# Gate column copied ahead of the masks, V three tiles ahead, query product first: a change to the prologue of a fused gated attention and feed-forward kernel

## The chip, the cores and the metric

The kernel runs on one core of one Trainium2 chip. The metric is the device time of one execution in microseconds (us), as the median of several executions. A run counts as slow, and is left out of the ratios, when it lies over 1.5% above the fastest of its kernel. The profiled span is about 2.0 to 2.3 us shorter than the time, because it runs from the first to the last recorded instruction of one execution.

## The reference

The input is x of 2048 rows and 512 columns (bf16). One branch is linear attention with 32 heads of 16, whose feature map is a pair of softmaxes; the other is a feed-forward layer with 1376 hidden units. A sigmoid gate mixes them.

```python
g = sigmoid((x * gate_w).sum(-1, keepdims=True))
# branch A
q, k, v = split(x @ wqkv)                      # 32 heads of 16
pq = einsum("bhsd,hdf->bhsf", q, w_phi)        # the same w_phi for k
phi_q = concat([softmax(pq), softmax(-pq)])    # phi_k alike
kv = einsum("bhsf,bhsd->bhfd", phi_k, v);  z = phi_k.sum(over s)
o = (phi_q @ kv) / (phi_q @ z + 1e-6)
a = o @ wo
# branch B
b = relu(x @ w1) @ w2
out = g * a + (1 - g) * b
```

## The kernel before

Each engine has its own list of instructions, executed in order; an event (`ev`) is a semaphore count that a later instruction waits for (`after`). The parts that matter here are all in the prologue. Three words are used throughout: a load "lands" when its data have arrived; a "bubble" is time by which a matmul starts later than the pace of its forerunners allows; "filler" is other work put where PE would wait. A hidden unit (`hunit`) and a V tile (`vtile`) are four matmuls of 512 columns each; the feed-forward layer takes eleven hidden units for 512 rows.

The loads go out from one queue (SP) in this order: x of the first 512 rows, W1 in pieces, the gate row, the rest of W1, the V weights (`WV`), the small w_phi (`WPS`), then the query and key weights **transposed** (`WQKT`), then the other rows of x.

```python
for dt in range(NDT):
    load_w1(1, dt)
p.dma("sp", ... GWR <- gate_w ..., ev="gwr")
p.dma("sp", ... W1[:, :, 1024:DFF] <- B_w1 ..., ev="w1r")
p.dma("sp", ... WV <- A_wqkv[:, 2 * D:3 * D] ..., ev="wv")
p.dma("sp", ... WPS <- A_w_phi ..., ev="wps")
p.dma("sp", lambda e: e.dma_start_transpose(out=WQKT, in_=A_wqkv[:, 0:2 * D]), "wqk", ev="wqk")
```

On DVE four block-diagonal masks times w_phi (`Wbd`) are emitted early, so they precede the gate column's copy, which makes the gate row a 97th column of the last hidden unit's weights:

```python
for gt in range(NDT):                       # emitted first
    p.op("dve", ... Wbd[:, gt, :] = WPS * M16 ..., after=["wps", "m16"], ev=f"wbd{gt}")
# ... cut ...
def gatecol():                              # emitted later
    p.op("pe",  ... transpose of GWR into PS[:, 3] ..., ev="gwt")
    p.op("dve", ... W1[:, :, DFF:DFF + 1] <- PS[:, 3] ..., after=["gwt"], ev="gw3")
```

`pre` multiplies the transposed weights with the masked w_phi, so that queries and keys come out of one projection already mapped ("merged weights"): eight groups of four small matmuls, the first four for queries, the last four for keys. Each group is copied out of PSUM (`pc0` to `pc7`), even ones by DVE and odd ones by ACT.

```python
def pre(half):
    PB = [0, 1, 2, 7]
    for i in range(4 * half, 4 * half + 4):
        # four matmuls  PS[:, PB[i % 4]] = WQKT * Wbd   after wqk, wbd0..3, a free bank
        # copy to WqP or WkP, ev=f"pc{i}"
```

The first tile of projections waits for all eight copies; query and key matmuls alternate. V tiles run two ahead.

```python
def atile(m):
    first = xready(m // 4) + ([f"em{m - 1}"] if m >= 1 else [f"pc{i}" for i in range(8)])
    pairs = [(dt, which) for dt in range(NDT) for which in (1, 0)]   # 1 = key, 0 = query
```

The order of PE work:

```python
hfirst(1, 0); gatecol(); hfirst(1, 1); hfirst(1, 2); hfirst(1, 3)
hunit(0, KTO[8])          # the hidden unit with the gate column, waits for gw3
hunit(0, KTO[9])
vtile(0)
pre(0)
hunit(0, KTO[10])
pre(1)
vtile(1)
for m in range(NT):       # 16 tiles
    atile(m)              # 8 matmuls, then exponentials (ACT), sums (DVE), scaling (POOL)
    if m >= LAG: kv(m - LAG)
    if m in vt: vtile(vt[m])
    for _ in range(nh[m]): hnext()     # one to three hidden units as filler
```

A tile with `nh[m] == 1` has its exponentials split so that the next tile's keys can start before its queries are done. After the loop come the products with kv, the output projections and the mixing.

The softmax here doesn't subtract the row's maximum and nothing guards it: scores larger than these inputs give would overflow.

## Time and profile before

| | before |
|---|---|
| median of runs | 153.9 us (153.61 to 153.94) |
| profiled span | 151.4 us |
| PE busy | 145.9 us, 96% of the span |
| first query/key projection starts | 20.44 us |

From the page of the kernel before: the span, the busiest engine, the busy tenths of the DMA engines in 40 slices of 3.8 us, and the chain of waits by engine.

```profile
span 151.4 us, 2399 instructions
...
PE 145.9 (96%) x925; PEld 73.9 (49%) x942; DVE 90.1 (59%) x147; ACT 79.8 (53%) x131; POOL 52.5 (35%) x57
...
DMA  4999993883533304333333311622223222332232
...
PE 87%; DMA 6%; SPq 4%; issue 1%; DVE 0%
```

PE is the bound, and the 16 DMA engines are 90% busy or more in the slices from 3.8 to 22.7 us, while the loads come in. Where PE stands idle is seen in its timeline. Columns: start in us, time in us, engine, line, operation, output<-inputs, shapes, number of merged instructions, and in brackets the idle time before it and what ended it.

```profile
10.22 0.17 PE L278 MATMUL PS<-IDN,GWR 4*128 4x4 bf16 x1
...
13.71 1.93 PE L258 MATMUL PS<-XT,W 128*97 128x512 bf16 x8 [0.61 <-DVE W L281]
15.47 1.03 PE L377 MATMUL PS<-WV,XT 128*128 128x512 bf16 x4
16.75 1.07 PE L294 MATMUL PS<-Wbd,PHQ 128*128 128x128 bf16 x16 [0.25 <-DMA PHQ<-in_A_wqkv_dram]
17.66 1.03 PE L258 MATMUL PS<-XT,W 128*128 128x512 bf16 x4
18.52 1.06 PE L294 MATMUL PS<-Wbd,PHQ 128*128 128x128 bf16 x16
19.63 0.81 PE L377 MATMUL PS<-WV,XT 128*128 128x512 bf16 x3
20.44 0.38 PE L321 MATMUL PS<-WkP,XT 128*128 128x512 bf16 x1
```

The timeline of DVE in the same stretch, the same columns:

```profile
12.67 0.90 DVE L234 TENSOR_TENSOR Wbd<-WPS,M 128x128 bf16<-128x128 bf16 x4 [5.22 <-DMA WPS<-in_A_w_phi_dram]
13.48 0.17 DVE L281 COPY W<-PS 128x4 bf16<-128x4 bf16 x1
```

The chain of waits of the kernel before, in order of time (start, length, what), around its last piece that is not PE:

```profile
7.42 9.28 DMA PHQ<-in_A_wqkv_dram
16.71 0.05 issue
16.75 1.07 PE PS L294 x16
```

How to read this. Matmuls of 512 columns start 0.216 us apart when nothing holds them, although each is shown as 0.38 us long. The Trainium skill (Perfetto Trace Analysis, "Tensor Engine Instruction") says that a matmul's end in a profile is estimated from its size and the memory's delay, not observed; the trace agrees in that matmuls which start 0.216 us apart are shown overlapping. So the idle time in brackets understates a bubble by 0.38 - 0.216 = 0.16 us. From start to start the bubbles are 0.77 us before 13.71 us (the gate copy on DVE, stuck behind four mask products that waited for w_phi until 12.67 us), 0.42 us before 16.75 us (the transposed load, which lands at 16.71 us), and 0.16 us before 20.44 us (the last copies of the merged weights). After that PE has no bubble until the tail. The V tile at 19.63 us shows three of its four matmuls: some records are missing from a trace (925 of PE here).

### The profile page before, as it was taken

What the parts mean: (1) busy time and instruction counts of PE and PEld (TensorE: products, weight loads), DVE (VectorE), ACT (ScalarE), POOL (GpSimd) and SP (SyncE); (2) the same over time, 40 slices, a digit from 0 to 9 for tenths busy, and PEclk for the clock granted to TensorE, in tenths of its full rate; (3) what the DMA queues carried; (4) which work ended last, traced back from release to release, by engine and by line L of the source; (5) the groups of instructions that cost most, each with busy time, mean ns of one, the idle gap of its engine ahead of it and who ended that gap; (6) DMA issues with size and microseconds to landing.
All of it is one profiled execution on the core that took longest, in us unless ns stands there. A gap on an engine that the chain in (4) does not pass through costs nothing.

```text
span 151.4 us, 2399 instructions
## 1 busy us (share of the span) xinstructions
PE 145.9 (96%) x925; PEld 73.9 (49%) x942; DVE 90.1 (59%) x147; ACT 79.8 (53%) x131; POOL 52.5 (35%) x57
## 2 busy tenths in 40 slices
PE   7998999999999999999999999999999999999993
PEld 2843544444445454444544445444444444445472
DVE  0502555777868786686688788455554555444462
ACT  3356649987787888878788763311222111111141
POOL 2000005987786686788668653000000000000000
PEclk9999999999999999999999999999999999999999
DMA  4999993883533304333333311622223222332232
GB/s 132 288 246 232 218 177 70 325 244 69 74 69 71 69 19 80 47 69 69 69 76 69 69 28 42 138 71 72 69 69 74 69 69 72 86 88 70 75 96 74
DMA packets 42130, 15.57 MB, mean 103 GB/s; under 512 B 37160, under 2 KB 41384, under 8 KB 42120
## 3 DMA queue, kind: packets, MB, share of 16 engines
q1 hardware_dynamic: 41448, 13.49, 40.5%
q0 software_dynamic: 528, 1.93, 3.7%
q8 instruction: 7, 0.11, 0.3%
q10 hardware_dynamic: 144, 0.01, 0.1%
q14 instruction: 3, 0.02, 0.0%
HBM read 4.41 MB, written 2.10 MB: 43 GB/s over the span
## 4 chain that ended last, share of the span: by engine, by line
PE 87%; DMA 6%; SPq 4%; issue 1%; DVE 0%
PE PS L467 23%; PE PS L258 19%; PE PS L321 18%; PE PS L479 9%; PE PS L377 8%; DMA PHQ<-in_A_wqkv_dram 6%; PE PS L438 3%; PE PS L399 3%; SPq L138 2%; PE PS L505 2%; PE PS L294 1%; PE PS L516 1%; SPq L148 1%; SPq L160 0%; SPq L158 0%
## 5 line engine op out<-in xcount | busy, mean ns | idle before, releaser
L467 PE MATMUL PS<-W,HT 128*128 128x512 bf16 (+1 forms) x159 | 37.6, 380 | 0.3
L258 PE MATMUL PS<-XT,W 128*128 128x512 bf16 (+1 forms) x142 | 34.3, 380 | 0.7 <-DVE W L281 0.6
L358 POOL TENSOR_TENSOR FM<-FM,SC 128x1024 bf16<-128x1024 bf16 x15 | 28.9, 1929 | 13.2 <-DVE SC L343 13.2
L484 ACT ACTIVATE TFA<-PS,GT 128x512 bf16<-128x512 f32 x15 | 10.3, 687 | 39.6 <-PE PS L479 39.6
L340 DVE TENSOR_REDUCE ZB<-FM 128x64 f32<-128x1024 bf16 x16 | 19.5, 1220 | 17.4 <-ACT FM L332 15.2
L273 ACT ACTIVATE HT<-PS 128x512 bf16<-128x512 f32 (+1 forms) x44 | 24.8, 608 | 8.6 <-PE PS L258 4.3
L332 ACT ACTIVATE FM<-PS 128x1024 bf16<-128x1024 f32 x22 | 21.3, 1021 | 10.1 <-PE PS L321 10.1
L467 PEld LDWEIGHTS PS<-W,HT 128*128 128x128 bf16 (+1 forms) x165 | 16.0, 98 | 19.6 <-ACT HT L273 0.3
L321 PE MATMUL PS<-WqP,XT 128*128 128x512 bf16 x64 | 22.3, 380 | 0.1
L321 PE MATMUL PS<-WkP,XT 128*128 128x512 bf16 x63 | 21.9, 379 | 0.0
L258 PEld LDWEIGHTS PS<-XT,W 128*128 128x128 bf16 (+1 forms) x144 | 14.0, 101 | 16.1 <-DVE W L281 1.1
L351 DVE TENSOR_REDUCE ZB<-FM 128x64 f32<-128x1024 bf16 x16 | 18.7, 1168 | 0.0
L363 POOL TENSOR_TENSOR FM<-FM,SC 128x512 bf16<-128x512 bf16 x16 | 16.9, 1054 | 1.3
L444 DVE RECIPROCAL RDEN<-PS 128x32 f32<-128x32 f32 x16 | 5.7, 357 | 17.6 <-PE PS L438 17.6
L490 DVE SCALAR_TENSOR_TENSOR OSB<-PS,OMG,TFA 128x512 bf16<-128x512 f32 x15 | 11.3, 751 | 7.1 <-ACT TFA L484 7.0
L377 PE MATMUL PS<-WV,XT 128*128 128x512 bf16 x58 | 15.1, 379 | 0.3
L479 PE MATMUL PS<-WO,OT 128*128 128x512 bf16 x59 | 15.0, 379 | 0.1
L337 ACT ACTIVATE FM<-PS 128x512 bf16<-128x512 f32 x20 | 10.3, 604 | 3.8 <-PE PS L321 3.8
L448 DVE TENSOR_TENSOR OTM<-PS,RDEN 128x512 bf16<-128x512 f32 x16 | 11.1, 691 | 0.6
L321 PEld LDWEIGHTS PS<-WkP,XT 128*128 128x128 bf16 x64 | 6.3, 98 | 7.9 <-DVE WkP L299 0.5
L321 PEld LDWEIGHTS PS<-WqP,XT 128*128 128x128 bf16 x64 | 6.3, 98 | 7.4
L343 DVE RECIPROCAL SC<-ZB 128x64 f32<-128x64 f32 x16 | 8.8, 553 | 0.5
(59 smaller groups left out, 106.5 us busy)
## 6 DMA issues: line engine op xcount, KB each, us to landing
out_dram<-OSB SPq DMA_DIRECT2D x15, 128.0 KB, 1.9
W<-in_B_w_dram POOLq DMA_DIRECT2D x1, 1280.0 KB, 6.6
W<-in_B_w_dram SPq DMA_DIRECT2D x8, 128.0 KB, 3.5
OT<-in_A_x_dram SPq DMA_DIRECT2D x2, 256.0 KB, 3.3
WV<-in_A_wqkv_dram SPq DMA_DIRECT2D x1, 512.0 KB, 6.0
WO<-in_A_wo_dram POOLq DMA_DIRECT2D x1, 512.0 KB, 7.0
W<-in_B_w_dram SPq DMA_DIRECT2D x1, 352.0 KB, 4.0
PHQ<-FM SPq DMA_TRANSPOSE x16, 2.7
```

The lines of the kernel that those rows point to most:

```text
L258: p.op("pe", lambda e, c=c, kt=kt, M=M, dt=dt, bank=bank: e.matmul(PS[0:M, bank, :], W1[:, dt, kt * P:kt * P + M], XT[:, dt, c * 512:(c + ...
L273: p.op("act", lambda e, c=c, kt=kt, Mr=Mr, bank=bank: e.activation(HT[0:Mr, kt, c * 512:(c + 1) * 512], PS[0:Mr, bank, :], ACT.Relu), afte ...
L321: p.op("pe", lambda e, m=m, dt=dt, which=which, W=(WqP, WkP)[which]: e.matmul(PS[:, which, :], XT[:, dt, m * P:(m + 1) * P], W[:, dt, :], ...
L332: p.op("act", lambda e, o=fm5[:, :, :, s, :], i=src, s=s: e.activation(o, i, ACT.Exp, scale=(1.0 if s == 0 else -1.0)), after=[f"qk{m}"] + ...
L340: p.op("dve", lambda e, b=b: e.tensor_reduce(ZB[:, b, 64:128], FM[:, b, 1, :].rearrange("p (g f) -> p g f", f=DH), AX.X, ALU.add), after=[ ...
L351: p.op("dve", lambda e, b=b: e.tensor_reduce(ZB[:, b, 0:64], FM[:, b, 0, :].rearrange("p (g f) -> p g f", f=DH), AX.X, ALU.add), after=[f" ...
L358: p.op("pool", lambda e, fk=fk, rk=rk: e.tensor_tensor(fk, fk, rk, ALU.mult), after=[f"rz{m}"], ev=f"pk{m}")
L363: p.op("pool", lambda e, b=b, fq=fq: e.tensor_tensor(fq, fq, SC[:, b, 0:32].unsqueeze(2).to_broadcast([P, H, DH]), ALU.mult), after=[f"sc{ ...
L377: p.op("pe", lambda e, m=m, dt=dt, bank=bank: e.matmul(PS[:, bank, :], XT[:, dt, m * P:(m + 1) * P], WV[:, dt, :], start=(dt == 0), stop=( ...
L467: p.op("pe", lambda e, kt=kt, M=M, m=m, bank=bank: e.matmul(PS[:, bank, :], HT[0:M, kt, m * P:(m + 1) * P], W2[0:M, kt, :], start=(kt == 0 ...
L479: p.op("pe", lambda e, t=t, m=m: e.matmul(PS[:, bank, :], OT[:, t, m * P:(m + 1) * P], WO[:, t, :], start=(t == 0), stop=(t == NDT - 1)), ...
L490: p.op("dve", lambda e, m=m, ob=ob: e.scalar_tensor_tensor(out=OSB[:, ob, :], in0=PS[:, BB[m % 3], :], scalar=OMG[:, m:m + 1], in1=TFA[:, ...
```

## The change

Its intent: to take the gate copy from behind the masks on DVE; to give PE work while it waits for the transposed load (a hidden unit before the merged weights, a third V tile after them); and to let the first projection begin with queries, which need only the first four copies. It needs a deeper V buffer (8 in place of 5), another assignment of PSUM banks, and it spreads the hidden units differently over the loop. The gate row's load goes out earlier (ahead of the second block of W1), and its transpose on PE comes four matmuls later.

```diff
@@
     GW = 128
     NB = 5
     NH = 3
+    NV = 8
     LAG = 3
 
     with ExitStack() as es:
@@
         W2 = E(nc.sbuf_tensor("W2", [P, KT, D], BF16))
         WO = E(nc.sbuf_tensor("WO", [P, NDT, D], BF16))
         FM = E(nc.sbuf_tensor("FM", [P, NB, 2, 2 * D], BF16))
-        VS = E(nc.sbuf_tensor("VS", [P, NB, NG, 68], BF16))
+        VS = E(nc.sbuf_tensor("VS", [P, NV, NG, 68], BF16))
         PHQ = E(nc.sbuf_tensor("PHQ", [P, NG, S], BF16))
         KVNZ = E(nc.sbuf_tensor("KVNZ", [P, NG, 68], BF16))
         OT = E(nc.sbuf_tensor("OT", [P, NDT, S], BF16))
@@
             load_w1(0, i)
         load_w1(0, 2)
         load_w1(0, 3)
+        p.dma("sp", lambda e: e.dma_start(out=GWR[:, :], in_=gate_w.rearrange("(j p) -> j p", p=P)), "gwr", ev="gwr")
         for dt in range(NDT):
             load_w1(1, dt)
-        p.dma("sp", lambda e: e.dma_start(out=GWR[:, :], in_=gate_w.rearrange("(j p) -> j p", p=P)), "gwr", ev="gwr")
         p.dma("sp", lambda e: e.dma_start(
             out=W1[:, :, 1024:DFF], in_=B_w1[:, 1024:DFF].rearrange("(j p) n -> p j n", p=P)), "w1r", ev="w1r")
         p.dma("sp", lambda e: e.dma_start(
@@
              after=["iota1", "r16"], ev="m16")
         p.op("dve", lambda e: e.tensor_tensor(M32[:, :], ROW32[:, 0:64], COL16[:, 0:64], ALU.is_equal),
              after=["r32"], ev="m32")
-        for b in range(NB):
+        for b in range(NV):
             p.op("dve", lambda e, b=b: e.memset(VS[:, b, :, 64:65], 1.0), ev=f"one{b}")
-        for gt in range(NDT):
-            wps_b = bass.AP(tensor=WPS, offset=gt * DH, ap=[[NDT * DH, P], [0, 8], [1, DH]])
-            p.op("dve", lambda e, gt=gt, a=wps_b: e.tensor_tensor(
-                Wbd[:, gt, :].rearrange("p (a b) -> p a b", a=8), a,
-                M16[:, :].rearrange("p (a b) -> p a b", a=8), ALU.mult),
-                after=["wps", "m16"], ev=f"wbd{gt}")
-
 
         hcount = [0]
 
@@
             p.op("dve", lambda e: e.tensor_copy(
                 W1[:, :, DFF:DFF + 1], PS[:, 3, 0:NDT].bitcast(BF16)[:, 0:NDT].unsqueeze(2)), after=["gwt"], ev="gw3")
 
+        def wbd():
+            # the four mask products removed above, unchanged
 
         def pre(half):
-            PB = [0, 1, 2, 7]
+            PB = [0, 1, 2, 7, 1, 2, 7, 3]
             for i in range(4 * half, 4 * half + 4):
                 which, dt = i // 4, i % 4
-                bank = PB[i % 4]
+                bank = PB[i]
                 dst = (WqP, WkP)[which]
-                after = ["wqk"] + [f"wbd{g}" for g in range(NDT)] + ([bfree[bank]] if i < 4 else [])
-                if i >= 4:
-                    after.append(f"pc{i - 4}")
+                after = ["wqk"] + [f"wbd{g}" for g in range(NDT)] + [f"pc{PB.index(bank)}" if PB.index(bank) < i else bfree[bank]]
                 for gt in range(NDT):
                     p.op("pe", lambda e, which=which, dt=dt, gt=gt, bank=bank: e.matmul(
                         PS[:, bank, gt * P:(gt + 1) * P], WQKT[:, which * NDT + gt, dt * P:(dt + 1) * P],
@@
                     p.op("act", lambda e, dst=dst, dt=dt, bank=bank: e.activation(
                         dst[:, dt, :], PS[:, bank, :], ACT.Copy), after=[f"pm{i}"], ev=f"pc{i}")
 
-        nh = [2, 2, 2, 2, 1, 2, 2, 1, 2, 2, 1, 2, 3, 1, 2]
+        nh = [2, 2, 2, 1, 2, 1, 2, 1, 2, 1, 2, 3, 3, 1, 2]
         split = [m for m in range(NT - 1) if nh[m] == 1] + [NT - 1]
 
         def atile(m):
@@
             if m >= 1:
                 first = first + [f"em{m - 1}"]
             else:
-                first = first + [f"pc{i}" for i in range(8)]
+                first = first + [f"pc{i}" for i in range(4)]
             after_split = m - 1 in split
             pairs = [(dt, which) for dt in range(NDT) for which in (1, 0)]
             if after_split:
                 pairs.sort(key=lambda t: -t[1])
                 first = [e for e in first if not e.startswith("em")] + [f"emk{m - 1}"]
+            mid = [f"em{m - 1}"] if after_split else ()
+            if m == 0:
+                pairs.sort(key=lambda t: t[1])
+                mid = [f"pc{i}" for i in range(4, 8)]
             for i, (dt, which) in enumerate(pairs):
                 p.op("pe", lambda e, m=m, dt=dt, which=which, W=(WqP, WkP)[which]: e.matmul(
                     PS[:, which, :], XT[:, dt, m * P:(m + 1) * P], W[:, dt, :],
                     start=(dt == 0), stop=(dt == NDT - 1)),
-                    after=(first if i == 0 else [f"em{m - 1}"] if after_split and i == NDT else ()),
+                    after=(first if i == 0 else mid if i == NDT else ()),
                     ev=(f"qk{m}" if i == 2 * NDT - 1 else None))
             fm5 = FM[:, b, :, :].rearrange("p a (h s f) -> p a h s f", h=H, s=2)
             src = PS[:, 0:2, :].rearrange("p a (h f) -> p a h f", h=H)
@@
                 f"tq{b}", after=[f"pq{m}"] + ([f"pm7"] if m == 12 else []), ev=f"tq{m}")
 
         def vtile(m):
-            b = m % NB
-            bank = 6 if m < 2 else 2
+            b = m % NV
+            bank = 6 if m < 3 else 2
             prev = [f"cv{m - 1}"] if m else [bfree[bank]]
-            if m == 2:
-                prev.append("pc6")
+            if m == 3:
+                prev.append("pc5")
             for dt in range(NDT):
                 p.op("pe", lambda e, m=m, dt=dt, bank=bank: e.matmul(
                     PS[:, bank, :], XT[:, dt, m * P:(m + 1) * P], WV[:, dt, :],
@@
                     after=((xready(m // 4) + ["wv"] + prev) if dt == 0 else ()),
                     ev=(f"v{m}" if dt == NDT - 1 else None))
             dst, src = VS[:, b, :, 0:64], PS[:, bank, :].rearrange("p (g c) -> p g c", g=NG)
-            after = [f"v{m}"] + ([f"kv{m - NB}"] if m >= NB else [])
-            if m < 2:
+            after = [f"v{m}"] + ([f"kv{m - NV}"] if m >= NV else [])
+            if m < 3:
                 p.op("dve", lambda e, d=dst, s=src: e.tensor_copy(d, s), after=after, ev=f"cv{m}")
             else:
                 p.op("act", lambda e, d=dst, s=src: e.activation(d, s, ACT.Copy), after=after, ev=f"cv{m}")
@@
             for g in range(NG):
                 after = []
                 if g == 0:
-                    after = [f"pka{m}" if m == NT - 1 else f"pk{m}", f"cv{m}", f"one{b}"]
+                    after = [f"pka{m}" if m == NT - 1 else f"pk{m}", f"cv{m}", f"one{m % NV}"]
                     if m == 0:
-                        after += ["cv1", "pc7"]
+                        after += ["cv2", "pc7"]
                 elif g == NG // 2 and m == NT - 1:
                     after = [f"pk{m}"]
                 p.op("pe", lambda e, m=m, b=b, g=g: e.matmul(
                     PS[:, 6 + g // 4, (g % 4) * GW:(g % 4) * GW + 65],
-                    FM[:, b, 1, g * P:(g + 1) * P], VS[:, b, g, 0:65],
+                    FM[:, b, 1, g * P:(g + 1) * P], VS[:, m % NV, g, 0:65],
                     start=(m == 0 and g % 4 == 0), stop=(m == NT - 1), skip_group_check=True),
                     after=after, ev=(f"kv{m}" if g == NG - 1 else f"kva{m}" if g == NG // 2 - 1 else None))
 
@@
         for kt in KTO[0:4]:
             hunit(0, kt, mm=False)
         hfirst(1, 0)
+        hfirst(1, 1)
         gatecol()
-        hfirst(1, 1)
+        wbd()
         hfirst(1, 2)
         hfirst(1, 3)
         for kt in KTO[4:8]:
@@
         hunit(0, KTO[8])
         hunit(0, KTO[9])
         vtile(0)
+        hunit(0, KTO[10])
         pre(0)
-        hunit(0, KTO[10])
+        vtile(1)
         pre(1)
-        vtile(1)
+        vtile(2)
+        bfree[3] = "pc7"
         units = [(c, kt) for c in range(1, NCH) for kt in [KT - 1] + list(range(KT - 1))]
-        vt = {m: m + 2 for m in range(NT - 4)}
+        vt = {m: m + 3 for m in range(NT - 5)}
         vt[NT - 3], vt[NT - 2] = NT - 2, NT - 1
 
         def hnext():
```

(Of the diff, the definition of the new `wbd()`, which holds the removed lines unchanged, and the line numbers are left out.)

More of the change, by code (lines that the diff above doesn't have):

```diff
@@ L282, in gatecol @@
                 W1[:, :, DFF:DFF + 1], PS[:, 3, 0:NDT].bitcast(BF16)[:, 0:NDT].unsqueeze(2)), after=["gwt"], ev="gw3")
+        def wbd():
+            for gt in range(NDT):
+                wps_b = bass.AP(tensor=WPS, offset=gt * DH, ap=[[NDT * DH, P], [0, 8], [1, DH]])
+                p.op("dve", lambda e, gt=gt, a=wps_b: e.tensor_tensor(
+                    Wbd[:, gt, :].rearrange("p (a b) -> p a b", a=8), a,
+                    M16[:, :].rearrange("p (a b) -> p a b", a=8), ALU.mult),
+                    after=["wps", "m16"], ev=f"wbd{gt}")
         def pre(half):
-            PB = [0, 1, 2, 7]
+            PB = [0, 1, 2, 7, 1, 2, 7, 3]
             for i in range(4 * half, 4 * half + 4):
                 which, dt = i // 4, i % 4
-                bank = PB[i % 4]
+                bank = PB[i]
                 dst = (WqP, WkP)[which]
-                after = ["wqk"] + [f"wbd{g}" for g in range(NDT)] + ([bfree[bank]] if i < 4 else [])
-                if i >= 4:
-                    after.append(f"pc{i - 4}")
+                after = ["wqk"] + [f"wbd{g}" for g in range(NDT)] + [f"pc{PB.index(bank)}" if PB.index(bank) < i else bfree[bank]]
                 for gt in range(NDT):
```

## The prediction

> What bounds the kernel. The profiled span is 151.4 us (153.9 us timed); the busy table puts PE at 96%, every other engine at 59% or less. In the timeline of PE, from the first query/key projection (20.44 us) on, matmuls of 512 columns start 0.216 us apart without a visible bubble; the chain of waits is almost all PE from 16.75 us. The Trainium skill (TensorE: Matmul & The Clock Gate, "Phases on the wall clock") gives about 216 ns per 512-column matmul back to back; the starts agree, and the 380 ns of the groups is latency. So only bubbles ahead of 20.44 us can be won.
>
> Bubbles there, from the starts of successive matmuls:
> 1. 12.93 to 13.71 us, 0.77 us: the hidden unit with the gate column waits for that column's copy (0.17 us), which sits on DVE behind four mask products (0.90 us), which wait until 12.67 us for their small weight load.
> 2. 16.34 to 16.75 us, 0.42 us: the merged weights wait for the transposed load of the query/key weights, landing at 16.71 us.
> 3. 20.28 to 20.44 us, 0.16 us: the first projection waits for the last copies of the merged weights (ACT, 20.29 us).
> Sum 1.35 us.
>
> What the change does. No matmul is added or removed. The gate copy now runs right after its transpose, about 11.3 us, well before 12.93; the mask products still end near 13.6 us, long before they are needed. Bubble 1 goes, but PE then meets the same landing of the transposed load, whose place in the queue is unchanged. A hidden unit (4 x 0.216 us) moves ahead as filler: work before the merged weights ends at 12.93 + 16 x 0.216 = 16.39 us, so bubble 2 stays at about 0.36 us. After 16.75 us, 32 small matmuls (0.056 us each) and two V tiles (0.86 us each) end at 20.27 us. Bubble 3 goes, because the query half needs only the first four copies (done about 18.5 us), and the key half starts 0.86 us later, when the others are done. I allow 0.05 us for V tile 2, which waits for the DVE copy of V tile 1 in the same bank.
> Before, the first projection started at 20.44 us with two V tiles done; after, at about 20.3 us with three. Gain: 0.14 + 0.86 = about 1.0 us, all on the critical path.
>
> Later parts. Six tiles instead of five have split exponentials. ACT in a one-unit iteration is about 2.06 + 0.6 + 0.6 us of 3.7 us of PE; POOL (1.93 + 0.25 + 1.05 us) and DVE (about 3.3 us) fit too. I expect no new bubble and no further gain.
>
> Prediction: 152.9 us, 8 in 10 between 152.3 and 153.5. Faster by over 2%: 0.02; within 2%: 0.96; slower by over 2%: 0.02.
>
> What would show it: no PE wait on the gate copy near 13 us; that copy ahead of the mask products on DVE; PE waiting about 0.36 us for the query/key weight load, still landing near 16.7 us; the first projection near 20.3 us, query first; then an unbroken chain and a span near 150.4 us.
>
> What would make it wrong: the transposed load landing at another time, which the merged weights follow one to one; a stall of V tile 2 or of the key half behind DVE copies; a wait on exponentials in the alternating one-unit iterations (3, 5, 7, 9), where ACT has least room; first-chunk matmuls waiting for weights now issued 0.4 us later, behind the gate row.

## The result, and the profile after

| | before | after |
|---|---|---|
| median of runs | 153.91 us (4 runs, 153.61 to 153.94) | 153.01 us (4 runs, 152.91 to 153.24) |
| profiled span | 151.4 us | 150.8 us |
| merged products start | 16.75 us | 17.13 us |
| first projection starts, V tiles done by then | 20.44 us, two | 20.72 us, three |

The ratio is 0.9948, with a 95% interval of 0.9931 to 0.9965: a small gain clear of the noise, well within 2%.

The page of the changed kernel, the same lines:

```profile
span 150.8 us, 2422 instructions
...
PE 146.5 (97%) x942; PEld 74.1 (49%) x942; DVE 90.8 (60%) x151; ACT 79.5 (53%) x132; POOL 52.6 (35%) x57
...
DMA  4999995793433319133333311622222223332232
...
PE 87%; DMA 6%; SPq 4%; issue 1%; DVE 0%
```

Its timeline of PE:

```profile
10.87 0.17 PE L272 MATMUL PS<-IDN,GWR 4*128 4x4 bf16 x1
...
12.71 1.89 PE L252 MATMUL PS<-XT,W 128*97 128x512 bf16 x8
14.44 1.03 PE L381 MATMUL PS<-WV,XT 128*128 128x512 bf16 x4
15.30 1.03 PE L252 MATMUL PS<-XT,W 128*128 128x512 bf16 x4
17.13 1.07 PE L294 MATMUL PS<-Wbd,PHQ 128*128 128x128 bf16 x16 [0.80 <-DMA PHQ<-in_A_wqkv_dram]
18.04 1.03 PE L381 MATMUL PS<-WV,XT 128*128 128x512 bf16 x4
18.90 1.06 PE L294 MATMUL PS<-Wbd,PHQ 128*128 128x128 bf16 x16
19.85 1.04 PE L381 MATMUL PS<-WV,XT 128*128 128x512 bf16 x4
20.72 1.03 PE L325 MATMUL PS<-WqP,XT 128*128 128x512 bf16 x4
21.59 1.03 PE L325 MATMUL PS<-WkP,XT 128*128 128x512 bf16 x4
```

Its timeline of DVE:

```profile
11.08 0.18 DVE L275 COPY W<-PS 128x4 bf16<-128x4 bf16 x1 [3.80 <-PE PS L272]
13.05 0.90 DVE L281 TENSOR_TENSOR Wbd<-WPS,M 128x128 bf16<-128x128 bf16 x4 [1.79 <-DMA WPS<-in_A_w_phi_dram]
```

Its chain of waits:

```profile
7.37 9.72 DMA PHQ<-in_A_wqkv_dram
17.09 0.05 issue
17.13 1.07 PE PS L294 x16
```

The gate copy now runs at 11.08 us, the gate unit at 12.71 us without a wait. The first projection begins with queries, at 20.72 us, and keys follow without a wait at 21.59 us. But the wait at the merged products is 0.97 us from start to start, not 0.36 us: the load landed at 17.09 us in this execution, 0.38 us later than in the profile of before, and PE reached the spot at 16.17 us, 0.22 us earlier than estimated. That is why the two spans differ by only 0.6 us while the medians differ by 0.9 us. Whether the later landing belongs to the change or to this one execution was the first question for the chip.

### The profile page after: what moved, and what is told of

Its sections match the earlier page's. It is cut to its first block, busy times and chain, and to the rows that moved or that the text cites. A ratio compares the mean times of both kernels' runs of the same rounds, so it can differ in the third digit from the quotient of the medians.

```text
span 150.8 us, 2422 instructions
## 1 busy us (share of the span) xinstructions
PE 146.5 (97%) x942; PEld 74.1 (49%) x942; DVE 90.8 (60%) x151; ACT 79.5 (53%) x132; POOL 52.6 (35%) x57
## 4 chain that ended last, share of the span: by engine, by line
PE 87%; DMA 6%; SPq 4%; issue 1%; DVE 0%
PE PS L471 24%; PE PS L252 19%; PE PS L325 18%; PE PS L381 9%; PE PS L483 9%; DMA PHQ<-in_A_wqkv_dram 6%; PE PS L442 3%; PE PS L403 3%; SPq L139 2%; PE PS L509 2%; PE PS L294 1%; PE PS L520 1%; SPq L149 1%; SPq L161 0%; SPq L159 0%
## 5 line engine op out<-in xcount | busy, mean ns | idle before, releaser
L471 PE MATMUL PS<-W,HT 128*128 128x512 bf16 (+1 forms) x165 | 38.1, 379 | 0.0
L336 ACT ACTIVATE FM<-PS 128x1024 bf16<-128x1024 f32 x20 | 19.4, 1021 | 8.6 <-PE PS L325 8.6
L325 PE MATMUL PS<-WkP,XT 128*128 128x512 bf16 x64 | 21.3, 379 | 0.0
L325 PE MATMUL PS<-WqP,XT 128*128 128x512 bf16 x64 | 21.3, 379 | 0.0
L381 PE MATMUL PS<-WV,XT 128*128 128x512 bf16 x64 | 16.4, 379 | 0.0
L341 ACT ACTIVATE FM<-PS 128x512 bf16<-128x512 f32 x24 | 12.4, 602 | 4.7 <-PE PS L325 4.7
L173 POOL DMA_DIRECT2D W<-in_B_w_dram x1 | 1.1, 1127 | 24.0 <-DMA XT<-in_A_x_dram 24.0
```

Of the source, the lines that this page charges most:

```text
L325: p.op("pe", lambda e, m=m, dt=dt, which=which, W=(WqP, WkP)[which]: e.matmul(PS[:, which, :], XT[:, dt, m * P:(m + 1) * P], W[:, dt, :], ...
L336: p.op("act", lambda e, o=fm5[:, :, :, s, :], i=src, s=s: e.activation(o, i, ACT.Exp, scale=(1.0 if s == 0 else -1.0)), after=[f"qk{m}"] + ...
L341: p.op("act", lambda e, o=fm5[:, which, :, s, :], i=src[:, which], s=s: e.activation(o, i, ACT.Exp, scale=(1.0 if s == 0 else -1.0)), afte ...
L381: p.op("pe", lambda e, m=m, dt=dt, bank=bank: e.matmul(PS[:, bank, :], XT[:, dt, m * P:(m + 1) * P], WV[:, dt, :], start=(dt == 0), stop=( ...
L471: p.op("pe", lambda e, kt=kt, M=M, m=m, bank=bank: e.matmul(PS[:, bank, :], HT[0:M, kt, m * P:(m + 1) * P], W2[0:M, kt, :], start=(kt == 0 ...
```

## The experiments

All kernels gave correct results. Theory A, from the prediction: the merged products start when the transposed load lands or when PE gets there, whichever is later, and nothing after them has a bubble in the new order. Its rivals are that each bubble is worth its own length, or that the change itself delays the load. Runs of one group shared a chip and its runs of the kernel before.

### The changed kernel again (after_again, no edit)

> The changed kernel once more, unedited, for the spread of the landing of the transposed query/key load. Theory A (the merged weights start at that landing and nothing after it has a bubble): the load lands somewhere between 16.6 and 17.2 us, the merged weights start 0.04 us later, the first projection 3.6 us after that; ratio to before 0.993 to 0.996. Rival (the change itself made the load land 0.4 us later, because the gate row now goes ahead of block 1): the landing stays at 17.1 us or later in every profile of a kernel with the gate row ahead.

Measured: 152.76 us (152.35 to 153.14), ratio 0.9902 (0.9847 to 0.9956). The ratio is below the one expected because five of the eleven runs of before on this chip lay near 155 us; against the other runs under 154 us (median 153.41 us) the gain is 0.65 us. The same line of PE's timeline as above:

```profile
16.50 1.07 PE L294 MATMUL PS<-Wbd,PHQ 128*128 128x128 bf16 x16
```

PE reached the merged products at 16.40 us by the count of starts and waited 0.10 us at most: the load had landed by 16.46 us, earlier than the 16.6 us expected, with the gate row ahead in the queue. So the rival, that the change makes the load land at 17.1 us or later, falls. In the other profiles that waited for the uncut load, the merged products started between 16.46 and 17.13 us with the gate row early, and between 16.75 and 16.88 us with it late. The second thing that moves is PE's arrival. In the profiles of before_again, old_units and split_load_2 (below) the matmuls' pace doubled (128 columns from 0.107 to 0.056 us apart) at about 3.9, 4.4 and 6.7 us. The Trainium skill (TensorE: Matmul & The Clock Gate, Part 1, "What's actually happening") says that the array's clock is held at half until a window of activity has passed, and that this window does not start with the kernel, so the moment varies from run to run. These traces agree that it varies; here it does so by 2.8 us, more than the half microsecond to either side that the page gives there. A late rise goes with a late arrival, though not strictly: the transpose of the gate row ran at 10.39 us in old_units (rise at 4.4 us), at 11.31 us in split_load_2 (6.7 us), but at 10.97 us in split_load (4.4 us). In the two profiles of the changed kernel the first projection started 0.63 us apart (20.72 and 20.09 us) and the spans differ by 0.6 us, so most of its spread of about 0.8 us can come from arrival and landing.

### Only the gate copy moved (gate_only)

```diff
-        # four mask products emitted before gatecol()
         gatecol()
         hfirst(1, 1)
+        # the same four mask products here
```

> The kernel before with only the four mask products moved behind the gate copy on DVE. Theory A: the 0.77 us wait at 12.93 us goes, PE reaches the merged weights at about 15.5 us and waits there 1.2 to 1.6 us for the transposed load instead of 0.4; the first projection starts where it did relative to the landing; time unchanged, ratio 0.999 to 1.001. Rival (the bubble is worth its own length): 0.77 us less, ratio 0.995.

Measured: 153.67 us, ratio 0.995 (0.9882 to 1.0018). 0.995 is the number of the rival, but the ratio cannot be used: this kernel's two runs at 155.6 and 155.8 us are left out of it as slow, while the runs of before near 155 us are in it. (More on this upper cluster below.) In the lower cluster (under 154 us) the median of before is 153.41 us (5 runs) and of this kernel 153.6 us (4 runs): no gain. PE's timeline:

```profile
12.73 1.89 PE L252 MATMUL PS<-XT,W 128*97 128x512 bf16 x8
...
16.88 1.07 PE L288 MATMUL PS<-Wbd,PHQ 128*128 128x128 bf16 x16 [1.40 <-DMA PHQ<-in_A_wqkv_dram]
```

The wait for the gate copy is gone (the gate unit runs at 12.73 us), and the wait at the merged products is 1.40 us in the bracket in place of 0.25. The first projection started at 20.57 us. The 0.77 us were handed on to the next wait, as theory A says.

### The gate copy put back behind the masks (no_gate)

```diff
-        gatecol()
         wbd()
+        gatecol()
```

> The changed kernel with the mask products back ahead of the gate copy. In both profiles the small weight load landed 4.04 us ahead of the transposed one. With the copy behind the masks PE starts the gate unit 1.04 us after the small load and reaches the merged weights 16 x 0.216 = 3.46 us later, 4.50 us after the small load, so it is 0.4 us late for the transposed load. Theory A: no wait at the merged weights, and 0.3 to 0.5 us slower than the changed kernel, ratio to before 0.997 to 0.998. Rival (the gate copy is worth its full 0.77 us or more): ratio 0.9995 or above. Rival (the gate copy is worth nothing, the filler is everything): ratio as the changed kernel, 0.9945.

Measured: 153.22 us (152.59 to 153.37), ratio 0.993 (0.987 to 0.999); on the same chip the changed kernel took 152.76 us. PE's timeline:

```profile
13.63 1.93 PE L252 MATMUL PS<-XT,W 128*97 128x512 bf16 x8 [0.74 <-DVE W L275]
...
17.12 1.06 PE L294 MATMUL PS<-Wbd,PHQ 128*128 128x128 bf16 x16
```

The gate unit waits again (0.74 us in the bracket, 0.90 us start to start), and the merged products start at 17.12 us with no wait, because PE is now later than the load. The cost is 0.46 us on medians (0.41 us on means, the runs of each spread over 0.8 us), within the 0.3 to 0.5 us of theory A; the profiles alone do not show it, since in the first one of the changed kernel the merged products also started at 17.13 us. The ratio, 0.993, is below the 0.997 expected because the mean of before held the upper cluster; on its lower cluster of 153.41 us the medians differ by 0.2 us, so the rest of the change without the early copy carries little. With the load uncut, the copy's early place is therefore worth about half of its bubble with the filler, and nothing measurable without it (gate_only).

### The transposed load cut in two (split_load, split_load_2)

```diff
-p.dma("sp", dma_start_transpose(out=WQKT, in_=A_wqkv[:, 0:2 * D]), ev="wqk")
+for w in range(2):        # query half, key half
+    p.dma("sp", dma_start_transpose(out=WQKT[:, w * NDT:(w + 1) * NDT, :],
+                                    in_=A_wqkv[:, w * D:(w + 1) * D]), ev=f"wqk{w}")
 # in pre():
-after = ["wqk"] + ...
+after = [f"wqk{which}"] + ...
```

> The changed kernel with the transposed load cut into a query half and a key half, each with its own semaphore, so that the first four merged products wait for the first half alone. Theory A: the query half lands near 13 to 15 us, the wait at the merged weights (0.97 us in the profile of the changed kernel, 0.4 by the blind estimate) goes, the key half lands near 17.1 us, ahead of the second four products at about 17.9 us; time 0.4 to 0.9 us below the changed kernel, ratio to before 0.989 to 0.992. Rival (the landing is not what bounds; something behind it, such as the copies, takes the time): ratio as the changed kernel, 0.9945.

Measured: 151.94 us (151.61 to 153.19), ratio 0.986 (0.9802 to 0.9919), 0.82 us below the changed kernel on the same chip. The execution that was profiled was the slowest of the six, at 153.19 us; PE's timeline of it:

```profile
16.27 1.06 PE L296 MATMUL PS<-Wbd,PHQ 128*128 128x128 bf16 x16
...
19.35 1.07 PE L296 MATMUL PS<-Wbd,PHQ 128*128 128x128 bf16 x16 [1.16 <-DMA PHQ<-in_A_wqkv_dram]
```

The query half made nobody wait, but the key half landed at 19.3 us. In the trace's DMA records a fetch of 16 KB of instructions ran from 16.65 to 18.30 us. No packet of the SP queue started between 17.33 and 18.29 us; after that they came one at a time, about 27 ns apart, until about 19.1 us, where the full stream of the next load set in. So it looks as if one of the 16 DMA engines had to finish the fetch before its share of the load; the records do not name the engine. The kernel was therefore run once more, unedited.

> The kernel with the split load once more, unedited, because its profiled run was its slowest by 1.1 us: the key half landed at 19.3 us, and a 16 KB instruction fetch took 1.65 us on the DMA engines just then. Expected: the key half lands before 18.5 us when no fetch meets it, the merged products then wait under 0.5 us in all, the first projection starts near 19.9 us, time near 151.9 us, 0.5 to 1.0 us below the changed kernel. Rival (cutting the load makes the key half late in itself): a wait of about 1.3 us at the second four products in this profile too.

Measured: 151.97 us (151.41 to 152.29), ratio 0.988 (0.9855 to 0.9906), on a chip where before took 153.74 us. PE's timeline:

```profile
16.61 1.06 PE L296 MATMUL PS<-Wbd,PHQ 128*128 128x128 bf16 x16
...
18.36 1.06 PE L296 MATMUL PS<-Wbd,PHQ 128*128 128x128 bf16 x16
```

No wait at either half; here the fetch came at 20.46 us, after both. PE's work runs without a bubble over 0.1 us from the gate unit at 13.15 us to the projection at 20.19 us. The landing was the bound of the changed kernel's prologue: in its five profiles with the uncut load and the early gate copy (after, after_again, old_units, no_third_v, no_query_first) the wait was 0.97, 0.10, 0.77, 0.75 and 1.29 us, 0.78 us on average, and cutting the load gained 0.82 us. Theory A holds and the rival (a half is late in itself) falls.

### The split load and the gate copy apart (split_only, gate_split)

split_only is the kernel before with the split load alone; gate_split has the split load and the gate copy ahead of the masks, and nothing else of the change.

> The kernel before with the masks behind the gate copy and the transposed load split, nothing else. The gate copy alone gave nothing measurable, as theory A says, because the landing took it back. With the landing of the query half out of the way it should now be worth something: PE reaches the merged weights at 15.5 us, waits up to 0.6 us for the query half, and the second four products wait for the key half at 17.3 us until 17.5 to 18.5 us; the first projection starts 0.3 to 1.0 us earlier than in before. Theory A: 0.3 to 0.8 us below the kernel before in runs of its lower cluster, about 152.8 us. Rival (the gate copy is worth nothing by itself, whatever the load does): as before, 153.4 us.

> The kernel before with the transposed load split and nothing else, to tell what the split is worth without the gate copy's early place. PE still waits for the gate copy until 13.7 us and reaches the merged weights at 16.34 us; the query half has landed by then, so only the 0.42 us wait there can go; the second four products are due at 18.1 us. Theory A: the first projection near 20.0 us against 20.4 to 20.6 in before, time 0.3 to 0.5 us below the lower cluster of before, about 153.0 us; then the gate copy's early place is worth a further 0.7 us or so in the kernel with both (152.3 us). Rival (the split did it all, the gate copy nothing): 152.3 us here too.

Measured: gate_split 152.33 us (151.8 to 154.91), ratio 0.9897 (0.9865 to 0.9928), before on that chip 153.74 us. split_only 153.21 us (152.32 to 153.45), ratio 0.9961 (0.9924 to 0.9998), before on its chip 153.57 us. PE's timeline of gate_split, then of split_only:

```profile
12.72 1.89 PE L254 MATMUL PS<-XT,W 128*97 128x512 bf16 x8
...
15.31 1.06 PE L290 MATMUL PS<-Wbd,PHQ 128*128 128x128 bf16 x16
...
17.07 1.06 PE L290 MATMUL PS<-Wbd,PHQ 128*128 128x128 bf16 x16
...
18.99 0.38 PE L317 MATMUL PS<-WkP,XT 128*128 128x512 bf16 x1
```

```profile
13.75 1.93 PE L260 MATMUL PS<-XT,W 128*97 128x512 bf16 x8 [0.40 <-DVE W L283]
...
16.38 1.06 PE L296 MATMUL PS<-Wbd,PHQ 128*128 128x128 bf16 x16
...
20.05 0.38 PE L323 MATMUL PS<-WkP,XT 128*128 128x512 bf16 x1
```

With both edits PE never waits for the gate copy or for either half, and the first projection starts at 18.99 us, against 20.05 us with the split alone (20.44 to 20.57 us in before and gate_only). Both halves thus landed in time for starts at 15.31 and 17.07 us. With the split alone only the wait at the merged products is gone (16.38 us, no bracket), and the time is 0.36 us below before, as expected. The gate copy, worth nothing measurable by itself, brings the start forward by 1.06 us here. Of that, 0.57 us is the bubble at the gate unit that split_only still has, from start to start; about 0.46 us is an earlier PE in that execution (the gate transpose ran at 10.02 us against 10.48 us). These two edits give more than the whole change (153.01 us), and nearly what the whole change gives with the split (151.97 us on the same chip). The gain of gate_split was larger than expected, and larger than the two bubbles that it removes (0.77 + 0.42 us by the profile of before); why is open. Its two upper runs (154.09 and 154.91 us) are left out of the ratio as slow and were not profiled; the median of the other four is 152.12 us.

### Without the third V tile (no_third_v), and without queries first (no_query_first)

```diff
 # no_third_v: V two tiles ahead, hidden units as in before
-        vtile(2)
-vt = {m: m + 3 for m in range(NT - 5)}
+vt = {m: m + 2 for m in range(NT - 4)}
 # ... cut: the bank, copy and wait conditions of V tile 2 as in before
 # no_query_first
-first = first + [f"pc{i}" for i in range(4)]
+first = first + [f"pc{i}" for i in range(8)]
-if m == 0: pairs.sort(key=lambda t: t[1]); mid = [pc4 .. pc7]
```

> The changed kernel with V two tiles ahead as before (and the order of hidden units of before, which that needs). Without the third V tile as filler the first projection starts 0.9 us earlier, its query half runs, and its key half waits for the last DVE copy of the merged weights, which ended 3.86 us after the merged products started in the profile of the changed kernel. Products, one V tile and the query half take 1.79 + 0.86 + 0.86 = 3.51 us: a wait of about 0.4 us, against 0.07 us of stalls with the filler. Theory A: 0.2 to 0.4 us slower than the changed kernel. Rival (the filler only moves work that the loop does anyway): same time.

> The changed kernel with the first projection interleaved as before, so that it waits for all eight copies of the merged weights. In the profile of the changed kernel it started 3.59 us after the merged products did, and the last copy ended 3.86 us after. Theory A: the projection starts 0.3 us later, time 0.2 to 0.4 us above the changed kernel. Rival (with a third V tile as filler the order of query and key is worth nothing): same time.

Measured: no_third_v 153.48 us (152.96 to 154.0), ratio 0.9955 (0.9904 to 1.0006); no_query_first 153.19 us (152.61 to 153.64), ratio 0.9936 (0.9879 to 0.9993). On the same chip the changed kernel with the old unit order (next section) took 152.92 us. The lines of PE's timeline where each waits, no_third_v first:

```profile
20.66 1.04 PE L325 MATMUL PS<-WkP,XT 128*128 128x512 bf16 x4 [0.23 <-DVE WkP L299]
```

```profile
20.82 0.39 PE L322 MATMUL PS<-WkP,XT 128*128 128x512 bf16 x1 [0.15 <-DVE WkP L299]
```

Each waits for the last DVE copy of the merged weights, the first for 0.39 us from start to start (0.605 us between starts where 0.216 are due), the second for 0.32 us (0.534 between starts). From the start of the merged products to the end of the first projection's stream, with the third V tile counted in for both, each needs 5.6 us, the changed kernel 5.3 us. So each profile shows 0.3 us of loss, as expected. On medians no_query_first loses 0.27 us, which six runs each, spread over 0.8 to 1.0 us, do not tell from nothing. no_third_v loses 0.56 us, more than expected: its profile shows one more wait, about 0.58 us ahead of the last output projection, for a transposed tile; whether its other runs had the same wait is open.

### The old order of hidden units (old_units)

```diff
-nh = [2, 2, 2, 1, 2, 1, 2, 1, 2, 1, 2, 3, 3, 1, 2]
+nh = [2, 2, 2, 2, 1, 2, 2, 1, 2, 2, 1, 2, 3, 1, 2]
```

> The changed kernel with the order of hidden units of the kernel before (one-unit iterations 4, 7, 10, 13 in place of 3, 5, 7, 9, 13). My theory (the order does nothing while PE is never idle in the loop): the time of the changed kernel within 0.2 us, no wait of PE in the loop. Rival (the alternating order is part of the gain): slower by 0.3 us or more, with waits on exponentials in the loop, or the upper cluster of the kernel before comes back.

Measured: 152.92 us (152.41 to 153.16), ratio 0.9915 (0.9865 to 0.9966); the changed kernel took 153.01 and 152.76 us on other chips. Its trace has one bubble in the loop, 0.22 us before the keys at 70.84 us. The new order is worth at most that by the trace, and the medians do not show it. The upper cluster did not come back in these six runs either.

### Queries in the middle (query_mid)

This is the split load with the first tile's query product moved between the two halves of the merged products.

> The split load, with the query half of the first tile moved between the two halves of the merged products, so that the key half of the load has 0.86 us more. The total of work is that of the split load. Expected: the second four products start near 19.0 us and wait at most 0.4 us even where the key half lands at 19.3; the first key projection starts near 20.8 us; time at or below that of the split load, 151.6 to 152.0 us, with a smaller spread. Rival (the split load has no wait left on its ordinary runs): equal within 0.1 us.

Measured: 151.98 us (5 runs, 151.8 to 152.45), ratio 0.989 (0.9865 to 0.9914), against 151.97 us for the split load on the same chip. Equal. That fits a split load without an ordinary wait, but does not show it: the profile of query_mid has two waits of its own for copies of the merged weights, 0.16 us before the query products and 0.12 us before the first key projection (20.58 us), which could hide a gain of that size.

### The kernel before again, and its upper cluster (before_again)

> The kernel before, unedited, once more: a null test of the ratio, and one more profile. On the last chip its eleven runs fell in two clusters, 153.3 to 153.5 and 154.9 to 155.4 us (one at 154.2), as did the kernel with only the gate copy moved; none of the 18 runs of the kernels built on the changed one did. Expected: ratio 1.000 within 0.005; if the profiled run falls in the upper cluster, its trace shows 1.7 us either as a later landing of the transposed load, or as a later rise of the TensorE clock near 6 us, or as a wait inside the loop.

Measured: 153.51 us (152.73 to 155.28), ratio 0.9952 (0.9887 to 1.0017) for identical code; so in groups with an upper cluster a ratio is good to half a per cent only. The profiled execution, at 155.28 us, was a slow one, so it says nothing of the change, but it shows what made this execution slow. Of the three guesses the last is the nearest: a wait of PE, but after the loop, at the first output projection. From its timeline and from its chain of waits:

```profile
99.95 1.02 PE L479 MATMUL PS<-WO,OT 128*128 128x512 bf16 x4 [1.55 <-DMA OT<-OTM]
```

```profile
95.28 4.53 DMA OT<-OTM
99.81 0.14 issue
99.95 1.02 PE PS L479 x4
```

The first output projection waits 1.55 us for the first transposed output tile. That tile's load took 4.53 us from issue to landing. The trace's DMA records show a 16 KB instruction fetch from 96.65 to 98.20 us, and the queue's next 41 packets only from 98.18 us on, again one at a time. In the fast profile of before the fetch came at 101.29 us, clear of these transfers. The Trainium skill (Runtime: NRT & Kernel Launch, "Instruction fetch mechanics") says that instructions are refilled by DMA in blocks of 16 KiB and that the cost of crossing a block, a step of the sequencer, is mostly hidden. What the traces of before_again and split_load show is another cost, which that section does not name: a data load that ran at the same time landed late. Of the 72 runs of the kernels with the old PE order (before, gate_only, split_only, gate_split) 17 were above 154.5 us; of the 51 of kernels built on the changed one none was above 154.0 us. In eight of the nine profiles of the latter the fetch at this stage lay between 98.2 and 99.7 us (in the other at 100.84 us). That a run of the upper cluster owes its time to this collision is seen in one execution (1.55 of about 1.7 us) and not tested by an edit. It need not be the only cause: the two upper runs of gate_only have a granted clock of 0.989 against at least 0.996 in every other run, which over 151 us is about 1.7 us by estimate. Why the fetch's moment varies more under the old order (96.65 to 101.29 us in five profiles) is open.

## Why the prediction was right

The time was: 152.9 us predicted, 153.01 us measured, within the range. The mechanism holds, but that the number is met to 0.1 us is in part luck (last points). Point by point:

- **PE the bound, only the prologue to win from.** Right. The changed profile has no PE bubble after 20.72 us, and the old unit order changed nothing that the medians show.
- **Bubble 1 goes but the landing takes it back.** Right, and shown by gate_only and gate_split: the gate copy alone left the time where it was and lengthened the next wait.
- **Bubble 2 "stays at about 0.36 us".** Mis-sized as a fixed term. In profiles of the changed order it was 0.97, 0.10 and, with small edits behind it, 0.75 to 1.3 us. I took both the landing (16.71 us) and PE's arrival (16.39 us) from one execution. Starts at the landing spread over 16.46 to 17.13 us and arrivals over 15.6 to 16.4 us. The sum does not contain this size: as long as both kernels wait for the same landing, the new order is ahead by one hidden unit of filler and bubble 3, less the allowance, 0.86 + 0.16 - 0.05 = 0.97 us. In the two profiles the landing differs by 0.38 us, and the gain from start to start is 0.86 - 0.28 = 0.58 us.
- **Bubble 3 goes.** Right: keys follow queries at 21.59 us without a wait, and without queries first a wait of 0.32 us is back. The allowance of 0.05 us for V tile 2 was right as well: it started 0.05 us after the merged products were through (0.95 us after their start of 18.90, where 0.90 are due).
- **Gain "about 1.0 us".** 0.9 us measured. The gain is not the sum of the bubbles (1.35 us), since the landing caps it. On other chips, against the runs of before under 154 us, it was less: 0.65 us (after_again) and 0.62 us (old_units against a median of 153.54 us). So the close hit on the first chip is partly luck; what takes the rest is open.
- **Not foreseen:** the upper cluster of the old order. On the chip of after_again, where five of eleven runs of before fell into it, it made the gain look like 1.0% in place of about 0.5%.

## What to carry to other kernels

When two waits follow each other and the second ends at a landing that the edit does not move, removing the first alone gains nothing; look at what the last arrival gates, and cut that transfer so that the first consumer waits only for its own part. Here this one edit gave about as much again as the whole reordering (0.8 us on top of 0.65 to 0.9 us), and with the DVE order it replaced most of it. Take the moment of a landing from several executions before building filler to its length.

## What the Trainium skill lacked or had wrong

- Runtime: NRT & Kernel Launch, "Instruction fetch mechanics", speaks of the cost of a refill to the sequencer alone and does not say that it can hold up data. Each execution here has seven fetches of 16 KB, of 0.9 to 2.4 us. During one an output tile came late and PE waited 1.55 us; during another the key half of a split load came late and PE waited 1.3 us between starts.
- TensorE: Matmul & The Clock Gate, Part 1, gives the moment of the clock's rise as varying by 500 ns to either side, and in another place by 6 to 14 slow matmuls; in these traces it lay between about 3.9 and 6.7 us. The page warns that the clock's events in a trace can be unreliable, but not that they can be missing before the rise: the granted-clock row reads 9 tenths in the first slice of before, where matmuls of 512 columns started 0.427 us apart, at half the later pace, and its first clock record is at 6.18 us.
- Perfetto Trace Analysis, "DMA Optimizations", says that splitting a transfer may let parts of it start sooner, and may help the whole where the DMA engines are generally idle. It does not treat a load in a busy queue, cut so that its first user waits for its own part only. Here they were 90% busy or more until 22.7 us in before, and the cut gained 0.82 us. It cost nothing measurable: both halves were there by 17.07 us in one profile, and uncut the load landed between 16.4 and 17.1 us.
